# Attention and GEGLU block: the order of the first attention units, and the first gate and value weights loaded by rows

## The chip, the core and the metric

One core of a Trainium2 chip runs the whole program. Its engines are TensorE (PE, with its weight loads listed apart as PEld), VectorE (DVE), ScalarE (ACT), GpSimd (POOL) and SyncE (SP); SP, ACT and POOL also hand transfers to the core's 16 DMA engines. The metric is the device time of one execution in microseconds (us).

## The reference

Eight batches of 576 tokens go through sliding-window attention with eight heads of width 64. Heads 0 to 3 see the last 32 positions ("plain"), heads 4 to 7 every fourth of the last 128 ("dilated"). The result, 4608 tokens of width 512, is the input of a GEGLU block.

```python
scores = scale * np.matmul(q, k.transpose(0, 1, 3, 2))
mask_plain = (rel >= 0) & (rel < window)                                             # window 32
mask_dil = (rel >= 0) & (rel < window * dilation) & (rel % dilation == 0)            # dilation 4
scores = np.where(masks[None, :, :, :], scores, -1000000000.0)
attn = np.exp(scores - max);  attn = attn / (sum(attn) + 1e-09)
x = np.matmul(attn, v).transpose(0, 2, 1, 3).reshape(B * S, H * D)
out = (gelu(x @ w_gate) * (x @ w_val)) @ w_out        # 512 -> 1536 -> 512, gelu with erf
```

## The kernel before

**Tiling.** A "unit" of attention is a pair of heads of one batch, so a batch has four: units 0 and 1 are plain, 2 and 3 dilated. Its steps are named by letters in strings that `run_program` reads one after another; each engine runs what it is given in that order, and nothing is moved by a scheduler. `c` casts q or k, `t` transposes them on PE and copies the result out of PSUM, `b` writes the mask as a bias into PSUM, `S` adds the scores, `P` takes the exponential on ACT, `D` sums it over the keys (matmuls with ones), `N` multiplies it with v, `X` (L608) multiplies N with the reciprocal of D and writes rows of xT, the transposed FFN input. The reciprocal is made in one of two ways: `T` and `B` (two 32x32 stream transposes and a reciprocal on DVE), or `l` and `r`, together `A` (logarithm and exponential of its negative, on ACT). `W` is a filler matmul that nobody reads. Of a word like `D2@20` the number behind `D` is the unit, and the one behind `@` tells the PSUM bank and the place in it.

**FFN.** Tokens come in nine chunks of 512. A chunk has 12 units of 128 hidden columns (nb); each takes four matmuls (kc = 0 to 3, by the 128 rows of xT) for the gate and four for the value (L617). `g` is the gelu on ACT (L776), `u` the product on DVE (L781). A digit word issues so many FFN matmuls from the chunk's list. xT[kc] is written by attention unit kc, so kc = 0, 1, 2, 3 need L608 of units 0, 1, 2, 3. The order of the first sixteen matmuls of chunk 0 (nb, gate or value, kc) is written out:

```python
orders = { 0: "000 100 002 102 010 110 012 112 001 101 011 111 003 103 013 113", ...
```

**Weights and v.** Gate and value weights are loaded in four parts each, by columns: 0 to 255, 256 to 511, and two of 512. POOL hands them to DMA and casts to half precision on the way (`load_w`), through the same instruction queue on which it casts v: v of units 0 and 1 of batch 0 comes by SP into `stage`, and POOL casts it into `vdiag`, where each head's values stand in one half of 128 columns and zeros, written by `zero` on DVE, in the other. One matmul with 128 columns of weights so serves both heads (L441), where units 2 and 3 use pairs of matmuls on a quarter of the array each (L452). POOL's transfers share eight semaphores; a transfer waits until the one eight before it has landed.

After the two batches' inputs and the three output weight tiles, chunk 0's second half (`out_words`) mixes the output matmuls (L624) with the attention of batch 1. From there on attention of the next batch always runs between output matmuls.

Of the kernel before, what the change touches and what calls it, by code (L numbers as in the profile page):

```python
# [9 lines left out]
F16 = mybir.dt.float16  # L10
F32 = mybir.dt.float32
# [10 lines left out]
def kernel(  # L22
# [23 lines left out]
    NKC = DM // P  # L46
# [5 lines left out]
    NB2 = S // BK  # L52
# [5 lines left out]
    const = ctx.enter_context(tc.tile_pool(name="const", bufs=1))  # L58
# [1 line left out]
    ldp = ctx.enter_context(tc.tile_pool(name="ldp", bufs=1))  # L60
    prb = ctx.enter_context(tc.tile_pool(name="prb", bufs=6))
    nrm = ctx.enter_context(tc.tile_pool(name="nrm", bufs=2))
    ffn = ctx.enter_context(tc.tile_pool(name="ffn", bufs=3))
    osbp = ctx.enter_context(tc.tile_pool(name="osbp", bufs=4))

    ones = const.tile([P, CH], F16, tag="ones")
# [7 lines left out]
    class_of = const.tile([P, 4], F16, tag="class_of")  # L74
    late_of = const.tile([P, P], F16, tag="late_of")

    WC = [(0, 256), (256, 512), (512, 1024), (1024, 1536)]
    wg_t = [const.tile([P, NKC, b - a], F16, tag=f"wg{i}", name=f"wg{i}") for i, (a, b) in enumerate(WC)]
    wv_t = [const.tile([P, NKC, b - a], F16, tag=f"wv{i}", name=f"wv{i}") for i, (a, b) in enumerate(WC)]
    wo_t = [const.tile([P, 4, DM], F16, tag=f"wo{i}", name=f"wo{i}") for i in range(3)]  # L80
    xT = [const.tile([P, NT], F16, tag=f"xT{i}", name=f"xT{i}") for i in range(NKC)]

    vraw = [const.tile([P, 4 * NB2 * D], F16, tag=f"v{i}", name=f"v{i}") for i in range(3)]
    vdiag = const.tile([P, 2 * NB2 * P], F16, tag="vdiag")
    qraw = [const.tile([P, 2 * QK], F16, tag=f"q{i}", name=f"q{i}") for i in range(2)]
    stage = const.tile([P, 3840], F32, tag="stage")
    s16 = const.tile([P, 4608], F16, tag="s16")
# [3 lines left out]
    ps = psum.tile([P, 8, 512], F32, tag="ps")  # L91
# [53 lines left out]
        rest_mask(nc.vector, rest)  # L145
        nc.vector.tensor_scalar(rest, rest, 1.0, BIG, ALU.subtract, ALU.mult)

    def load_w(*parts):

        for i in parts:  # L150
            for t, w in ((wg_t, moe_w_gate), (wv_t, moe_w_val)):
                src = w[:, WC[i][0] : WC[i][1]].rearrange("(kc p) n -> p kc n", p=P)
                nc.gpsimd.dma_start(out=t[i], in_=src)

    def load_wo(i):
        return nc.gpsimd.dma_start(
# [11 lines left out]
    def rows_in(src, r):  # L168

        return src.rearrange("h (p r) d -> p h (r d)", r=r)  # L170
# [15 lines left out]
    def at2(t, c0, dims):  # L186
        base = t[:, c0 : c0 + 1]
        return bass.AP(tensor=base.tensor, offset=base.offset, ap=[base.ap[0]] + dims)

    diag = vdiag.rearrange("p (e c) -> p e c", c=P)  # L190

    def zero():

        for x in range(2):
            nc.vector.memset(at2(vdiag[64 * x : 64 * x + 64].bitcast(F32), 32 - 32 * x, [[64, 2 * NB2], [1, 32]]), 0.0)

    def st_of(i):
        return stage[:, 1280 * i : 1280 * i + 1280]
# [48 lines left out]

        return nc.gpsimd.tensor_copy(dst, st_of(i)[:, 0:1152].rearrange("p (e d) -> p e d", d=D))  # L248

    def cast_diag(g):  # L250

        st = st_of(0)[:, 0:1152].rearrange("p (e d) -> p e d", d=D)
        at = slice(NB2 * g, NB2 * g + NB2)
        for x in range(2):
            nc.gpsimd.tensor_copy(diag[half_of(x), at, half_of(x)], st[half_of(x), at])

    def half_of(x, swap=0):
        y = x ^ (1 if swap else 0)
        return slice(64 * y, 64 * y + 64)

    def odd(n):

        return n % 2 if n >= NHP else 0
# [137 lines left out]
    def win(n, at):  # L401

        bank, kind = at // 10, at % 10
        return 512 * bank + ((0, 832, 960, 0) if is_plain(n) else (80, 880, 880, 64))[kind]
# [34 lines left out]
    def emit(mms):  # L439
        for o, lhs, rhs, st, end in mms:  # L440
            nc.tensor.matmul(o, lhs, rhs, start=st, stop=end, skip_group_check=True)  # L441

    def emit_tiles(*lists):

        queues, at = [list(mms) for mms, _ in lists], [0.0] * len(lists)
        while any(queues):
            i = min((i for i in range(len(lists)) if queues[i]), key=lambda i: at[i])
            o, lhs, rhs, st, end = queues[i].pop(0)
            at[i] += max(int(np.prod(rhs.shape[1:])), 72)
            for x in range(2):  # L450
                rows, cols = half_of(x), half_of(x, lists[i][1])
                nc.tensor.matmul(o[cols], lhs[rows], rhs[rows], start=st, stop=end, skip_group_check=True)  # L452
# [91 lines left out]
    def two_num_mms(n, i):  # L544
        b, hp = n // NHP, n % 2
        _, _, _, _, vp, vd = tiles["two", b]
        tiles["num", n] = win(n, i)
        if is_plain(n):
            vp = vp if b else diag
            return two_mms(n, win(n, i), lambda e: vp[:, NB2 * hp + e, :])  # L550
        return two_mms(n, win(n, i), lambda e: vd[:, NB2 * hp + (8 if e is None else e % 2 * 4 + e // 2), :])

    def two_den(n, i):
# [5 lines left out]

    def two_num(n, i):  # L560
        mms = two_num_mms(n, i)
        if n < NHP and is_plain(n):
            emit(mms)
        else:
            emit_tiles((mms, odd(n)))
# [44 lines left out]
    def ffn1_part(c, nb, gi, bank, kcs):  # L610

        tok = slice(c * CH, (c + 1) * CH)
        i = next(i for i, (_, end) in enumerate(WC) if nb * P < end)
        ns = slice(nb * P - WC[i][0], nb * P - WC[i][0] + P)
        w = (wg_t, wv_t)[gi][i]
        for kc, first, end in kcs:
            nc.tensor.matmul(ps[:, bank, :], w[:, kc, ns], xT[kc][:, tok], start=first, stop=end)  # L617

    def parts_of(order):
        return [(kc, i == 0, i == len(order) - 1) for i, kc in enumerate(order)]  # L620
# [41 lines left out]
    def warm(n, bank, rows=P, cols=CH):  # L662

        for _ in range(n):
            nc.tensor.matmul(ps[0:rows, bank, 0:cols], ones[:, 0:rows], ones[:, 0:cols], start=True, stop=True)
# [14 lines left out]
    for h in range(0, HK, 2):  # L680
        for t, src, eng in ((0, q, nc.sync), (1, k, nc.scalar)):
            first = eng.dma_start(out=first_p[:, t, h : h + 2], in_=rows_in(src[0, h : h + 2], 6))
# [9 lines left out]
    v_cast(0, 1)  # L692
    tiles["two", 0] = views(0)

    warm(69, 7, 32, 32)
    warm(4, 7)
    nc.vector.tensor_reduce(class_of, ident.rearrange("p (i r) -> p r i", r=4), axis=mybir.AxisListType.X, op=ALU.max)
    biases()
    zero()
    bias_first(0, 4)  # L700
    load_w(0, 1)
    for g in range(2):
        cast_diag(g)
    load_w(2)

    def second():
# [17 lines left out]
    def gate_banks(c, nb):  # L724

        if c == 0:
            return ((4, 5), (6, 7))[nb] if nb < 2 else ((0, 1), (2, 3))[nb % 2]
        return ((0, 7), (1, 6) if c == 1 else (1, 4))[nb % 2]

    def gate_list(c):  # L730

        if c in firsts:
            first, seen = [], {}
            for word in firsts[c].split():
                nb, gi, kc = (int(x) for x in word)
                i = seen[nb, gi] = seen.get((nb, gi), 0) + 1
                first.append((nb, gi, (kc, i == 1, i == NKC)))
        else:
            first = [(nb, gi, part) for nb in range(2) for gi in range(2) for part in parts_of(range(NKC))]
        order = [(nb, gi) for nb in range(2, NNB) for gi in range(2)]  # L740
        if c == 0:
            order = [(nb + n, gi) for nb in range(2, 10, 2) for gi in range(2) for n in range(2)] + order[16:]
        rest = [(nb, gi, part) for nb, gi in order for part in parts_of(range(NKC))]
        return [lambda m=m: ffn1_part(c, m[0], m[1], gate_banks(c, m[0])[m[1]], [m[2]]) for m in first + rest]

# [60 lines left out]
    def gate_words(c):  # L806

        if c == 0:
            return (
# [4 lines left out]
            )  # L814
        loads = {1: "F3", 2: "R", 3: "F5 H5", 4: "F6 H6", 5: "F7 H7"}.get(c, "")
        rest = " ".join(f"4 g{nb} 4 u{nb}" for nb in range(2, NNB - 1))
        if c == 1:
            return f"{loads} 8 G 3 g0 1 u0 3 g1 1 u1 {rest} 4 g{NNB - 1} 4"
        before = f"e3@{c - 1}" if c < NCH - 1 else ""
        return f"{before} {loads} 7 G 3 g0 1 u0 1 g1 4 u1 {rest} 4 g{NNB - 1} 4" + (f" u{NNB - 1}" if c > 6 else "")  # L820

    def out_words(c):
# [16 lines left out]
        )  # L839

    orders = {
# [43 lines left out]
```

## Time and profile before

| what | before |
|---|---|
| device time, median of 3 | 327.19 us (327.05 to 327.22) |
| the profiled execution, its device time | 326.98 us |
| its span, first to last instruction | 325.3 us |
| granted TensorE clock over the span | 1.000 |
| DVE busy | 150.2 us, 46% |
| ACT busy | 159.6 us, 49% |
| instructions of PE's matmul row | 3207 |
| first FFN matmul starts | 17.74 us |
| fifth FFN matmul starts, the first with value weights | 19.05 us |
| the last of the four L608 of batch 0 ends | 20.40 us |

Times within an execution count from the span's start. The profile page gives each engine's busy time, the span in 40 slices of 8.1 us with the granted clock (PEclk) and the share of DMA in tenths, and the chain of work that ended last. The timeline lists instructions in order: start, duration, engine, source line, operation, tiles written and read, how many, and in brackets how long the engine sat idle before and what ended that. The profiled execution is one of its own, so its device time differs a little from the median; the step from its span to its device time is what lies around the program's first and last instruction.

### The profile page before, as it was taken

The numbers are of one execution on the slowest core, as the hardware profiler recorded it, in microseconds if no ns is written. First come the engines' busy times: TensorE is split into PE (matmuls) and PEld (weight loads), VectorE is DVE, ScalarE is ACT, GpSimd is POOL, SyncE is SP. The second block draws the span as 40 slices with busy tenths as digits, with TensorE's granted clock in tenths as the row PEclk, the third lists the DMA queues.
The fourth block names the chain that finished last, engine by engine and source line by source line (L and its number), as shares of the span: only waits on it lengthen the run. The fifth ranks groups of instructions, "written<-read, shape, count | busy, mean of one in ns | idle before, by whom it ended". The sixth has DMA issues, their size and how long they took to land.

```text
span 325.3 us, 7737 instructions
## 1 busy us (share of the span) xinstructions
PE 318.9 (98%) x3207; PEld 155.8 (48%) x3207; DVE 150.2 (46%) x226; ACT 159.6 (49%) x240; POOL 82.3 (25%) x134
## 2 busy tenths in 40 slices
PE   6999999999999999999999999999999999999996
PEld 4754544445444445445444544445444544444443
DVE  6864636444644464346533554355434644204410
ACT  2662577435753556346633863376435753233321
POOL 8785603402482512332033201411000000000000
PEclk9999999999999999999999999999999999999999
DMA  8999998988799999897489537972000200020002
GB/s 190 188 188 206 201 191 165 269 180 199 171 271 208 240 169 245 197 222 191 119 201 232 141 104 157 253 173 90 32 2 8 94 33 0 2 99 30 0 34 97
DMA packets 106659, 47.11 MB, mean 145 GB/s; under 512 B 83584, under 2 KB 102144, under 8 KB 106624
## 3 DMA queue, kind: packets, MB, share of 16 engines
q1 hardware_dynamic: 93120, 38.29, 50.0%
q0 software_dynamic: 12944, 7.67, 16.7%
q10 hardware_dynamic: 560, 0.66, 0.7%
q8 instruction: 25, 0.41, 0.6%
q14 instruction: 10, 0.08, 0.1%
HBM read 37.75 MB, written 9.44 MB: 145 GB/s over the span
## 4 chain that ended last, share of the span: by engine, by line
PE 61%; ACT 0%; DVE 0%; issue 0%; ACTq 0%
PE ps L617 38%; PE ps L624 19%; PE ps L452 3%; PE ps L648 1%; ACT lg L579 0%; DVE osb L657 0%; ACTq L579 0%
## 5 line engine op out<-in xcount | busy, mean ns | idle before, releaser
L781 DVE SCALAR_TENSOR_TENSOR u_all<-g,ps 128x512 f16<-128x512 f16 x108 | 74.2, 688 | 110.0 <-PE ps L617 93.3
L776 ACT ACTIVATE g<-ps 128x512 f16<-128x512 f32 x108 | 63.6, 597 | 104.1 <-PE ps L617 104.1
L617 PE MATMUL ps<-xT,wg 128*128 128x512 f16 x432 | 112.5, 379 | 0.3 <-DMA wg<-in_moe_w_gate_dram 0.3
L617 PE MATMUL ps<-xT,wv 128*128 128x512 f16 x432 | 112.3, 379 | 0.0
L624 PE MATMUL ps<-wo,u_all 128*128 128x512 f16 x420 | 96.3, 380 | 0.0
L617 PEld LDWEIGHTS <-wv 128*128 128x128 f16 x432 | 42.1, 98 | 51.1 <-DMA wv<-in_moe_w_val_dram 0.7
L617 PEld LDWEIGHTS <-wg 128*128 128x128 f16 x432 | 42.1, 98 | 50.7 <-DMA wg<-in_moe_w_gate_dram 0.4
L624 PEld LDWEIGHTS <-u_all 128*128 128x128 f16 x420 | 39.1, 98 | 45.5 <-issue 0.5
L608 DVE TENSOR_TENSOR xT<-ps,rb 128x576 f16<-128x576 f32 x32 | 28.8, 938 | 16.9 <-PE ps L452 13.6
L482 ACT ACTIVATE P<-ps 128x832 f16<-128x832 f32 (+1 forms) x32 | 25.3, 835 | 15.4 <-PE ps L452 15.3
L211 POOL CAST s<-stage 128x640 f16<-128x640 f32 x24 | 17.4, 752 | 51.0 <-DMA stage<-in_q_dram 37.9
L248 POOL CAST v<-stage 128x1152 f16<-128x1152 f32 x11 | 12.7, 1151 | 63.0 <-DMA stage<-in_v_dram 47.4
L579 ACT ACTIVATE lg<-ps 128x576 f32<-128x576 f32 x30 | 18.7, 653 | 11.6 <-DVE xT L608 9.0
L637 DVE TENSOR_SCALAR osb<-ps 128x512 f32<-128x512 f32 x22 | 15.1, 686 | 12.2 <-PE ps L624 11.6
L585 ACT ACTIVATE rb<-lg 128x576 f32<-128x576 f32 x30 | 19.5, 690 | 0.3
L635 ACT ACTIVATE osb<-ps 128x512 f32<-128x512 f32 x13 | 7.8, 598 | 21.2 <-PE ps L624 21.2
L223 POOL CAST s<-stage 128x512 f16<-128x512 f32 x24 | 14.4, 627 | 10.1 <-DMA stage<-in_q_dram 7.9
L487 DVE TENSOR_TENSOR P<-P,two_d 128x768 f16<-128x768 f16 x14 | 9.4, 678 | 9.8 <-ACT P L482 9.1
L487 DVE TENSOR_TENSOR P<-P,two_p 128x832 f16<-128x832 f16 x14 | 8.6, 612 | 9.5 <-ACT P L482 9.5
L803 ACT ACT_TABLE_LOAD x9 | 11.5, 1283 | 0.2
L452 PEld LDWEIGHTS <-v 64*64 64x64 f16 x616 | 7.6, 107 | 6.3 <-issue 5.7
L452 PEld LDWEIGHTS <-q 64*64 64x64 f16 x576 | 7.9, 107 | 5.0 <-issue 3.0
(67 smaller groups left out, 135.6 us busy)
## 6 DMA issues: line engine op xcount, KB each, us to landing
out_dram<-osb SPq DMA_DIRECT2D x35, 256.0 KB, 2.8
stage<-in_v_dram SPq DMA_DIRECT2D x28, 144.0 KB, 3.8
stage<-in_q_dram SPq DMA_DIRECT2D x24, 128.0 KB, 3.6
stage<-in_k_dram SPq DMA_DIRECT2D x24, 128.0 KB, 2.9
stage<-in_q_dram SPq DMA_DIRECT2D x6, 512.0 KB, 4.7
stage<-in_k_dram SPq DMA_DIRECT2D x6, 512.0 KB, 5.3
stage<-in_v_dram SPq DMA_DIRECT2D x20, 128.0 KB, 2.8
wo<-in_moe_w_out_dram POOLq DMA_DIRECT2D x3, 512.0 KB, 16.8
```

The source lines that it names most:

```text
L211: nc.gpsimd.tensor_copy(s16[:, 1280 * t + 640 * g : 1280 * t + 640 * g + 640].rearrange("p (k c) -> p k c", k=5), st_of(i).rearrange("p (k ...
L452: nc.tensor.matmul(o[cols], lhs[rows], rhs[rows], start=st, stop=end, skip_group_check=True)
L482: nc.scalar.activation(pt[:, 0 : src.shape[1]], src, AF.Exp, bias=0.0, scale=scale)
L487: tiles["M"] = nc.vector.tensor_tensor(pt, pt, mask, ALU.mult)
L579: nc.scalar.activation(lg, psf[:, c0 : c0 + S], AF.Ln)
L585: nc.scalar.activation(rb, tiles.pop(("lg", n)), AF.Exp, scale=-1.0)
L608: nc.vector.tensor_tensor(dst, num, rb, ALU.mult)
L617: nc.tensor.matmul(ps[:, bank, :], w[:, kc, ns], xT[kc][:, tok], start=first, stop=end)
L624: nc.tensor.matmul(ps[:, bank, :], u_all[:, fc, tb * P : (tb + 1) * P], wo_t[fc // 4][:, fc % 4, :], start=(fc == 0), stop=(fc == NNB - 1),)
L637: nc.vector.tensor_scalar(osb, ps[:, bank, :], 1.0 / USCALE, None, ALU.mult)
L776: nc.scalar.activation(g, ps[:, gate_banks(c, args[0])[0], :], AF.Gelu)
L781: nc.vector.scalar_tensor_tensor(u_all[:, nb, :], tiles.pop(("g", nb)), USCALE, val, ALU.mult, ALU.mult)
```

## The change

Four things change, all in the work ahead of and inside the first chunk.

1. The words of chunk 0 are in another order: casts and transposes of unit 0 and 1's second tensors (`c2 c3 t2 t3`) and of unit 2 come together, before the sums of unit 0; unit 3's sums, logarithm and reciprocal come ahead of the values of units 0, 2 and 3; L608 runs for units 0, 2, 3, 1. Unit 1's reciprocal goes from `T`, `B` to `l`, `r`. Eleven of twelve filler matmuls go. The warm-up is 46 matmuls of 32 columns and 12 of 64 where it was 69 of 32.
2. v of unit 0 is cast densely (one cast), and its values use pairs of matmuls as units 2 and 3 do; only unit 1 keeps `vdiag`, which is half as large, and so is what `zero` clears.
3. The first 512 columns of the gate and value weights come by rows: gate rows of kc = 0 and kc = 2 in a transfer each (256 KB of the 4-byte source each), value rows of kc = 0 and 2, then gate rows of 1 and 3, then value rows of 1 and 3. On POOL's queue the cast of unit 0's v stands between the first value and the second gate part, the casts of unit 1's v before the second value part.
4. The written order of chunk 0 covers the first four units: gate of units 0 to 3 comes before the value of units 2 and 3; their PSUM banks change, and g has four buffers where it had three.

```diff
-    ffn = ctx.enter_context(tc.tile_pool(name="ffn", bufs=3))
+    ffn = ctx.enter_context(tc.tile_pool(name="ffn", bufs=4))
...
-    WC = [(0, 256), (256, 512), (512, 1024), (1024, 1536)]
...
+    wg_t = [const.tile([P, NKC // (1 if i > 1 else 2), CH], F16, tag=f"wg{i}", name=f"wg{i}") for i in range(4)]
+    wg_t[0] = [const.tile([P, CH], F16, tag=f"wg0{i}", name=f"wg0{i}") for i in range(2)]
+    wv_t = [const.tile([P, NKC // (1 if i > 1 else 2), CH], F16, tag=f"wv{i}", name=f"wv{i}") for i in range(4)]
...
-    vdiag = const.tile([P, 2 * NB2 * P], F16, tag="vdiag")
+    vdiag = const.tile([P, NB2 * P], F16, tag="vdiag")
...
+    def load_w(i, *kinds):
+
+        for gi in kinds or (0, 1):
+            t, w = ((wg_t, moe_w_gate), (wv_t, moe_w_val))[gi]
+            cols = w[:, CH * max(i - 1, 0) : CH * max(i - 1, 0) + CH]
+            if i > 1:
+                nc.gpsimd.dma_start(out=t[i], in_=cols.rearrange("(kc p) n -> p kc n", p=P))
+            elif i == 0 and gi == 0:
+                for n in range(2):
+                    nc.gpsimd.dma_start(out=t[i][n], in_=cols[2 * n * P : 2 * n * P + P, :])
+            else:
+                nc.gpsimd.dma_start(out=t[i], in_=cols.rearrange("(a b p) n -> b p a n", b=2, p=P)[i])
...
-            nc.vector.memset(at2(vdiag[64 * x : 64 * x + 64].bitcast(F32), 32 - 32 * x, [[64, 2 * NB2], [1, 32]]), 0.0)
+            nc.vector.memset(at2(vdiag[64 * x : 64 * x + 64].bitcast(F32), 32 - 32 * x, [[64, NB2], [1, 32]]), 0.0)
...
-    def cast_diag(g):
...
+    def cast_first(g):
+
+        if g == 0:
+            nc.gpsimd.tensor_copy(vraw[0][:, 0:576], st_of(0)[:, 0:576])
+            return
+        st = st_of(0)[:, 576:1152].rearrange("p (e d) -> p e d", d=D)
         for x in range(2):
-            nc.gpsimd.tensor_copy(diag[half_of(x), at, half_of(x)], st[half_of(x), at])
+            nc.gpsimd.tensor_copy(diag[half_of(x), :, half_of(x)], st[half_of(x)])
...
-    warm(69, 7, 32, 32)
+    warm(46, 7, 32, 32)
+    warm(12, 7, 32, 64)
     warm(4, 7)
...
-    load_w(0, 1)
-    for g in range(2):
-        cast_diag(g)
+    load_w(0)
+    cast_first(0)
+    load_w(1, 0)
+    cast_first(1)
+    load_w(1, 1)
     load_w(2)
...
-            return ((4, 5), (6, 7))[nb] if nb < 2 else ((0, 1), (2, 3))[nb % 2]
+            return ((4, 2), (5, 3), (6, 7), (0, 1))[nb] if nb < 4 else ((0, 1), (2, 3))[nb % 2]
...
-                "c0@0 c1@0 t0@0@1 t1@1@0 b1@6 W1@3@0 S0@4 P0 t4@0@1 W1@3@0 c2@0 c3@0 t5@1@0 t2@2@1 t3@3@0 D0@40 T0 B0 "
-                "t6@1@1 W10@7 t7@0@0 S1@6 P1 b2@2 S2@2 P2 D1@60 T1 B1 b3@0 S3@0 P3 D2@20 A2 N0@40 X0 D3@00 N2@60 X2 A3 N3@20 1 "
-                "N1@00 X1 X3 G V 15 g0 u0 g1 u1 4 g2 4 g3 4 u2 4 u3 4 g4 4 g5 4 u4 4 u5 4 g6 4 g7 4 u6 4 u7 4 g8 4 g9 4 u8 3 "
+                "c0@0 c1@0 t0@0@1 t1@1@0 b1@6 W1@3@0 S0@4 P0 c2@0 c3@0 t4@0@1 t2@2@0 t3@3@1 t5@1@0 D0@40 T0 B0 S1@6 P1 b2@2 S2@2 P2 "
+                "t6@0@1 t7@1@0 D1@60 l1 r1 b3@0 S3@0 P3 D2@20 l2 r2 D3@00 l3 r3 N0@40 X0 N2@20 X2 N3@60 X3 2 N1@00 X1 G V 11 g0 1 g1 4 g2 2 g3 3 u0 1 u1 4 u2 4 u3 "
+                "4 g4 4 g5 4 u4 4 u5 4 g6 4 g7 4 u6 4 u7 4 g8 4 g9 4 u8 3 "
...
-        0: "000 100 002 102 010 110 012 112 001 101 011 111 003 103 013 113",
+        0: "000 100 002 102 010 110 012 112 200 202 003 103 001 101 300 302 203 201 303 301 013 113 011 111",
```

Behind the written order the value matmuls of units 2 and 3 follow, and from unit 4 on the list is as before. Everything after chunk 0's first half stands in the same order in both kernels.

More of the change, by code (lines that the diff above doesn't have):

```diff
@@ L75 @@
     late_of = const.tile([P, P], F16, tag="late_of")
-    WC = [(0, 256), (256, 512), (512, 1024), (1024, 1536)]
-    wg_t = [const.tile([P, NKC, b - a], F16, tag=f"wg{i}", name=f"wg{i}") for i, (a, b) in enumerate(WC)]
-    wv_t = [const.tile([P, NKC, b - a], F16, tag=f"wv{i}", name=f"wv{i}") for i, (a, b) in enumerate(WC)]
+    wg_t = [const.tile([P, NKC // (1 if i > 1 else 2), CH], F16, tag=f"wg{i}", name=f"wg{i}") for i in range(4)]
+    wg_t[0] = [const.tile([P, CH], F16, tag=f"wg0{i}", name=f"wg0{i}") for i in range(2)]
+    wv_t = [const.tile([P, NKC // (1 if i > 1 else 2), CH], F16, tag=f"wv{i}", name=f"wv{i}") for i in range(4)]
     wo_t = [const.tile([P, 4, DM], F16, tag=f"wo{i}", name=f"wo{i}") for i in range(3)]
@@ L146, in biases @@
         nc.vector.tensor_scalar(rest, rest, 1.0, BIG, ALU.subtract, ALU.mult)
[L148 to L153, printed above, removed]
+    def load_w(i, *kinds):
[9 more added lines that the diff above has]
+                nc.gpsimd.dma_start(out=t[i], in_=cols.rearrange("(a b p) n -> b p a n", b=2, p=P)[i])
     def load_wo(i):
@@ L248, in cast_v @@
         return nc.gpsimd.tensor_copy(dst, st_of(i)[:, 0:1152].rearrange("p (e d) -> p e d", d=D))
-    def cast_diag(g):
-        st = st_of(0)[:, 0:1152].rearrange("p (e d) -> p e d", d=D)
-        at = slice(NB2 * g, NB2 * g + NB2)
+    def cast_first(g):
[3 more added lines that the diff above has]
+        st = st_of(0)[:, 576:1152].rearrange("p (e d) -> p e d", d=D)
         for x in range(2):
-            nc.gpsimd.tensor_copy(diag[half_of(x), at, half_of(x)], st[half_of(x), at])
+            nc.gpsimd.tensor_copy(diag[half_of(x), :, half_of(x)], st[half_of(x)])
     def half_of(x, swap=0):
@@ L548, in two_num_mms @@
         if is_plain(n):
-            vp = vp if b else diag
-            return two_mms(n, win(n, i), lambda e: vp[:, NB2 * hp + e, :])
+            return two_mms(n, win(n, i), lambda e: diag[:, e, :] if n == 1 else vp[:, NB2 * hp + e, :])
         return two_mms(n, win(n, i), lambda e: vd[:, NB2 * hp + (8 if e is None else e % 2 * 4 + e // 2), :])
@@ L561, in two_num @@
         mms = two_num_mms(n, i)
-        if n < NHP and is_plain(n):
+        if n == 1:
             emit(mms)
@@ L612, in ffn1_part @@
         tok = slice(c * CH, (c + 1) * CH)
-        i = next(i for i, (_, end) in enumerate(WC) if nb * P < end)
-        ns = slice(nb * P - WC[i][0], nb * P - WC[i][0] + P)
-        w = (wg_t, wv_t)[gi][i]
+        ns = slice(nb % 4 * P, nb % 4 * P + P)
+        ws = (wg_t, wv_t)[gi]
         for kc, first, end in kcs:
-            nc.tensor.matmul(ps[:, bank, :], w[:, kc, ns], xT[kc][:, tok], start=first, stop=end)
+            w = ws[nb // 4 + 1][:, kc] if nb > 3 else (ws[0][kc // 2] if kc % 2 + gi == 0 else ws[kc % 2][:, kc // 2])
+            nc.tensor.matmul(ps[:, bank, :], w[:, ns], xT[kc][:, tok], start=first, stop=end)
     def parts_of(order):
@@ L737, in gate_list @@
                 first.append((nb, gi, (kc, i == 1, i == NKC)))
+            assert set(seen.values()) == {NKC}
         else:
@@ L741, in gate_list @@
         if c == 0:
-            order = [(nb + n, gi) for nb in range(2, 10, 2) for gi in range(2) for n in range(2)] + order[16:]
+            order = [(2, 1), (3, 1)] + [(nb + n, gi) for nb in range(4, 10, 2) for gi in range(2) for n in range(2)] + order[16:]
         rest = [(nb, gi, part) for nb, gi in order for part in parts_of(range(NKC))]
```

## The prediction

> **What bounds the kernel now.** First the busy table, the row of slices and the chain that ended last.
>
> ```profile
> PE 318.9 (98%) x3207; PEld 155.8 (48%) x3207; DVE 150.2 (46%) x226; ACT 159.6 (49%) x240; POOL 82.3 (25%) x134
> ...
> PEclk9999999999999999999999999999999999999999
> DMA  8999998988799999897489537972000200020002
> ...
> PE 61%; ACT 0%; DVE 0%; issue 0%; ACTq 0%
> PE ps L617 38%; PE ps L624 19%; PE ps L452 3%; PE ps L648 1%; ACT lg L579 0%; DVE osb L657 0%; ACTq L579 0%
> ```
>
> The chain is matmuls alone. It goes back only to 122 us, where one wait cuts it, so I looked further back in the order of instructions. From 19.05 us to the end one matmul of 512 columns follows another every 0.2158 us; all that is lost is some 0.09 us where the array changes tile shape, and 0.3 us at 122.4. Nothing behind 19 us can be gained by this change; it can only move the point where that stream opens, or tear a hole into it. So the stretch around the opening decides.
>
> ```profile
> 15.69 0.44 PEld L441 LDWEIGHTS <-vdiag 128*128 128x128 f16 x10 [0.38 <-POOL vdiag L255]
> ...
> 17.67 0.74 POOL L153 DMA_DIRECT2D wg<-in_moe_w_gate_dram  x1
> 17.73 0.10 PEld L617 LDWEIGHTS <-wg 128*128 128x128 f16 x1 [0.39 <-DMA wg<-in_moe_w_gate_dram]
> 17.74 0.39 PE L617 MATMUL ps<-xT,wg 128*128 128x512 f16 x1 [0.30 <-DMA wg<-in_moe_w_gate_dram]
> ...
> 18.36 0.81 PE L617 MATMUL ps<-xT,wg 128*128 128x512 f16 x3
> ...
> 18.60 1.79 DVE L608 TENSOR_TENSOR xT<-ps,rb 128x576 f16<-128x576 f32 x2 [0.30 <-PE ps L441]
> 19.05 0.55 PEld L617 LDWEIGHTS <-wv 128*128 128x128 f16 x4 [0.38 <-DMA wv<-in_moe_w_val_dram]
> ...
> 26.82 1.42 PEld L617 LDWEIGHTS <-wv 128*128 128x128 f16 x8 [0.31 <-DMA wv<-in_moe_w_val_dram]
> 26.84 1.89 PE L617 MATMUL ps<-xT,wv 128*128 128x512 f16 x8
> ```
>
> The reader is to see three waits for weights: the first gate weights (17.7), the first value weights (19.05, the fifth FFN matmul), and the third value part wv2 (26.82, the 41st), where only the load of weights waits. The attention (L608) is no longer what is waited for at 19.05. The landing events in the trace say the same: wg0 17.69, wv0 19.01, wg1 20.32, wv1 21.65, wg2 24.25, wv2 26.77. PE and the weight transfers run neck and neck: 36 matmuls x 0.2158 = 7.77 us from 19.05 give 26.82.
>
> **Attention front.** Replayed with the durations of the timeline:
> - `zero` halves: two memsets of 0.54 us become about 0.28 each. The first cast stood right behind them (5.47), its data landed at 4.82, so unit 0's scores go from 7.86 to about 7.35. This is lost again at unit 2's transposes, which wait for their DMA until 8.44 (idle 0.15 before them now).
> - Order: second pair's casts and transposes ahead, and of 12 filler matmuls (L671: 1 + 1 + 10) one is left, so 0.22 + 0.67 us go. Transposes then end at 9.5, their four copies (0.64 on ACT, 0.76 on DVE, two on each) at 10.2 and 10.8; scores of unit 1 at 10.25 (12.14 before), exp to 11.7; unit 2's exp to 12.6.
> - Unit 1's transposed reciprocal (0.77 + 0.27 + 0.78 on DVE) becomes log and exp on ACT (0.65 + 0.68). ACT then is the attention's engine: copy to 13.1, log and exp of unit 1 to 14.45, exp of unit 3 to 15.27 (15.83 before), logs and exps of unit 2 to 16.5 and of unit 3 to 17.8 (18.34 before).
> - Unit 0's v dense: 10 matmuls 128x96 (0.40 us) become 20 half-array ones (40 take 0.75, so 0.37): nothing. On POOL two 64x576 casts (0.68, 0.66) become one 128x576 (about 0.70, by 0.75 for 128x640). It needs the stage's second piece, behind which today's second cast starts at 14.98; so values of unit 0 start at 15.74 (15.69 now).
> - L608 runs in the order 0, 2, 3, 1: 16.35 to 17.1 (0.76 us, a plain one), to 18.16 (1.13, a dilated one), to 19.2, to 19.9. All four ended at 20.40 before. The matmuls of chunk 0 need pair 2 as third and fourth: 18.22; so the fifth could start at 18.65.
>
> All this gains 0.4 us at the fifth matmul, **if the weights were there**.
>
> **Weights.** The first four FFN matmuls still need gate weights only, and the fifth still a value part, with which 512 KB (as landed) are in, as now. So its landing doesn't come nearer by the split. Packets grow from 512 B to 1 KB: in the trace 256 KB of 512 B packets take 1.32 us (the steps between the landings above), 512 KB of 1 KB packets 2.52 to 2.60, so 1.27 per 256 KB. From the last v landing at 16.35: wg first halves 17.0 and 17.6, wv0 18.89, wg1 20.16, wv1 21.43. Fifth matmul at 18.93: **-0.12 us** (the 41st then could start at 26.70, -0.14). The rule in the Trainium skill that speaks against splitting (DMA: Bandwidth & Descriptors, "Measured": batch to 1 MiB or more; "Anatomy of one DMA": about 2.0 us fixed per transfer) would put up to 2.0 us on the one transfer more. The row says zero as long as transfers are queued: landings 1.32 apart, without a gap. I take zero there, but the fixed part comes back where the queue runs dry.
>
> And there it can: POOL now casts between the weights. Today all four first parts are handed over by 14.17; only wg2 comes behind the casts (17.67), and the DMA packet records show the price: 95 KB landed per half microsecond, then 41 and 76 KB in those from 19.5 and 20.0, so full rate some 2.1 us after the hand-over and 0.43 us lost on the mean engine. After: wg1 15.65, wv1 17.73 (its two diag casts wait for stage pieces of 16.04 and 17.0 as today), wg2 18.46, wv2 19.20. Most engines end wv0 near 16.95 and idle 0.4 to 0.85 us, then 0.4 to 0.8 before wv1; today's 0.43 goes. They have that to give: 15 of 16 finish wg0 by 16.31, the last at 17.69, and that last engine, 1.4 us behind all through, never runs dry. So wv2 lands near 26.55 on the last engine and 26.15 to 26.55 on the rest. PE asks for it at 18.93 + 36 x 0.2158 = 26.70. Bound from below: no hole.
>
> On top comes PE's own instruction fetch (the queue named instruction, 25 packets of 16 KB): one took 0.96 us at 22.99, and one engine's wg2 came 0.8 us behind its neighbours. It follows PE's count of instructions; 12 fewer matmuls ahead of it move it by 12 x 0.216 = 2.6 us to about 25.5, into the tail of wv2, on an engine whose lead is now used up: 26.9 to 27.3. Then the 41st matmul starts at 26.95 to 27.35 against 26.84: **+0.1 to +0.5**. I take 27.05, +0.2, as the fetch may miss wv2.
>
> **The rest.** Order and banks of hidden units (nb) 0 to 3: each bank's former reader (L608 at the latest 19.9; the gate and product rows of 0.60 and 0.69) ends before its next matmul; nb 4's gate in bank 0 at 25.0 wants nb 3's gelu, over by 23.5. The fourth buffer of g removes what the four gates in a row would wait for. Zero. Later weights: wg3 is due at 31.9 (29.27 now), the first output weights at 41.70 (41.37 now): 0.33 us of cover, the thinnest; the fetch at 39.21 that delays it also moves back. Warm-up 46 x 27 ns + 12 x 27 to 53 ns is what 69 x 27 ns was, and PE waits behind it anyway.
>
> **Clock.** Taking fillers out speaks against the Trainium skill (TensorE: Matmul & The Clock Gate, last table: no PE gaps over about 3 us; one idle window of 3.4 us halves the clock). My largest gap is 1.1 us (12.3 to 13.46). The row: from 5.3 to 8.7 us matmuls other than transposes fill only 0.9 us and the clock stays at 9; after the change the leanest 3.4 us (12.0 to 15.4) hold 1.37. By the row nothing; if the gate closed, 3.4 us at half rate cost 1.7.
>
> **Sum.** Profiled execution 326.98 (span 325.3, 1.7 around it): -0.14 from the opening, +0.35 at wv2 (27.05 against 26.70), so +0.2, 327.18. The median shown is 0.21 above that execution: **327.4**. A difference under 0.2% (0.65 us) this measurement can't tell from none; that is where I expect it.
>
> **Rivals and chances.**
> - Forecast, weights pace both ends, 326.9 to 327.8: 72%.
> - The lagging engine lags less (its 1.4 us come from the 1.5 us fetch at 9.6, which moves too), the fifth matmul starts at 18.65 and wv2 is in time: -0.4, 326.8; with L608 earlier still, under 326.5. For: attention has slack. Against: fetches keep coming. 9%, half of it beyond 0.2%.
> - Slower: the queue dries out on the lagging engines too. Place: wv1 and wv2; decides once hand-over to full rate is above 2.5 us (wv1 then starts after 20.2, where the last engine ends wg1). With the fetch on top wv2 lands at 27.7 to 28.1: +0.9 to +1.3, 328.3. 14%.
> - Clock gate closes in the front: +1.7, 328.9. 5%.
> Range 326.7 to 328.2: the rest outside is about 2 in 10. Faster 5%, same 76%, slower 19%.
>
> **What would show it.** Right: the fifth FFN matmul waits for wv at 18.8 to 19.0, L608 ends before 20.1, a wait for wv near 26.7 to 27.3. Wrong: the fifth matmul waits for L608; no wait at wv2; a PEclk digit under 9 in the second or third slice; a hole at the first output matmul.

## The result and the profile after

The changed kernel takes **328.09 us** (median of 8 runs, 327.56 to 329.06), the kernel before beside it 327.14 us (8 runs, 326.89 to 327.78): a ratio of 1.0029, with an interval of 1.0019 to 1.0039. That is 0.95 us slower, with the whole interval above 1. The time lies inside the range given, but it is the place and the size of the third rival, not of the forecast. The profiled execution of the changed kernel took 328.04 us, its span is 326.3 us.

The page of the changed kernel first: the busy table, the granted clock and the DMA share in slices, and the chain that ended last, by engine and by line.

```profile
PE 318.6 (98%) x3195; PEld 155.3 (48%) x3195; DVE 148.2 (45%) x223; ACT 160.6 (49%) x242; POOL 81.9 (25%) x134
...
PEclk9999999999999999999999999999999999999999
DMA  8999999998899997896589627972000200020002
...
PE 93%; DMA 4%; DVE 1%; issue 1%; POOL 0%; ACT 0%
```

The source lines have moved: what was L608 (writes of xT) is L615 in the changed kernel, the FFN's L617 is L624, the output matmuls' L624 is L631, and L441 and L452 are L449 and L460 (experiments 2 and 8, on the kernel before, keep the old lines).

PE, DVE and POOL are busy for 0.3 to 2.0 us less than before, ACT for 1.0 us more (unit 1's reciprocal is made there now), and the clock is untouched, so the loss is idle time on PE. What is new is the 4% of DMA in the chain: 9.02 us of it (2.8%) are the transfer of wv2, the rest is a load of q before 8.7 us. Before, the chain was cut at 122 us and held matmuls almost alone; now it can be followed to the start. The chain of waits in order of time (start, length, what) names the new piece:

```profile
17.89 1.11 DVE xT L615
19.00 9.02 DMA wv<-in_moe_w_val_dram
28.07 8.59 PE ps L624 x39
```

From 19.00 to 28.02 the end of the program waits for one transfer: wv2, from POOL's hand-over to its landing. (That a DVE instruction stands before it is inferred by the profile; POOL itself has no idle time there, as its hand-over before took from 18.25 to 19.01.) Behind it PE runs as before. The timeline of the changed kernel (start, duration, engine, line, operation, count, in brackets the idle time before and what ended it) shows how POOL came to hand it over at 19.00, and what PE did meanwhile:

```profile
13.69 0.33 PE L449 MATMUL ps<-P,two_ones 128*128 128x288 f16 x3 [0.77 <-issue]
14.84 0.66 POOL L259 CAST v<-stage 128x576 f16<-128x576 f32 x1 [2.29 <-DMA stage<-in_v_dram]
15.45 0.73 POOL L159 DMA_DIRECT2D wg<-in_moe_w_gate_dram  x1
16.18 1.41 POOL L263 CAST vdiag<-stage 64x576 f16<-64x576 f32 x2
17.21 3.50 DVE L615 TENSOR_TENSOR xT<-ps,rb 128x576 f16<-128x576 f32 x4 [3.55 <-PE ps L460]
17.53 0.72 POOL L159 DMA_DIRECT2D wv<-in_moe_w_val_dram  x1
...
19.00 0.75 POOL L154 DMA_DIRECT2D wv<-in_moe_w_val_dram  x1
19.49 1.02 PE L624 MATMUL ps<-xT,wv 128*128 128x512 f16 x4
...
28.07 0.60 PE L624 MATMUL ps<-xT,wv 128*128 128x512 f16 x2 [0.64 <-DMA wv<-in_moe_w_val_dram]
```

Three things are to be seen. POOL sits 2.29 us in front of the first cast, waiting for v, and behind that cast stand wg1 and, after two more casts, wv1. The fifth FFN matmul starts at 19.49 where it was 19.05. And until 28.07 PE waits for wv2 (the 41st FFN matmul, 26.84 before): 1.23 us later, and the 96th is 1.24 later, the span 1.08.

How much the DMA engines moved in the two stretches in question is in the windows view: stretch, length, busy time and count of PE, PEld, DVE, ACT, POOL, then the clock, the DMA share and GB/s. The kernel before:

```profile
16.50:18.00 1.50, 1.20 (x46) 1.00 (x43) 1.38 (x2) 1.47 (x3) 1.20 (x3) 1.00 1.44 199
18.50:20.00 1.50, 1.50 (x9) 0.57 (x7) 1.40 (x2) 1.14 (x1) 1.50 (x3) 1.00 1.29 155
```

The changed kernel:

```profile
16.50:18.00 1.50, 1.41 (x64) 1.38 (x63) 0.79 (x2) 1.38 (x3) 1.44 (x3) 1.00 0.89 130
18.50:20.00 1.50, 1.44 (x16) 0.87 (x15) 1.50 (x3) 1.48 (x2) 1.50 (x3) 1.00 0.63 73
```

In both stretches the rate is lower than before, 130 against 199 and 73 against 155 GB/s: POOL's transfers had run dry. The packet records of that one queue say the same in KB per half microsecond, and the landing events say what it cost. All 16 DMA engines report each transfer; the median of the 16 tells of the queue, the last of the 16 is what PE waits for.

```
KB per 0.5 us from   16.5 17.0 17.5 18.0 18.5 19.0 19.5 20.0
before                 95   92   95   95   98   93   41   76
changed                54   51   74   97   46   26   38   93

landed, us            wv0          wg1          wv1          wg2          wv2
               median last  median last  median last  median last  median last
before          17.14 19.01  18.46 20.32  19.78 21.65  22.91 24.25  25.52 26.77
changed         17.05 18.86  19.03 20.14  21.44 22.28  24.31 24.82  26.91 28.02
```

Against 95 KB per half microsecond the changed kernel lacks 281 KB, the one before 75 KB. Before, the median engine was 1.25 to 1.87 us ahead of the last one; in the changed kernel that lead melts, and at wg2 it is 0.51.

### The profile page after: what moved, and what is told of

Same layout as the page of the kernel before. It is cut to its first block, busy times and chain, and to the rows that moved or that the text cites. A ratio compares the mean times of both kernels' runs of the same rounds, so it can differ in the third digit from the quotient of the medians.

```text
span 326.3 us, 7703 instructions
## 1 busy us (share of the span) xinstructions
PE 318.6 (98%) x3195; PEld 155.3 (48%) x3195; DVE 148.2 (45%) x223; ACT 160.6 (49%) x242; POOL 81.9 (25%) x134
## 3 DMA queue, kind: packets, MB, share of 16 engines
q0 software_dynamic: 11936, 7.67, 16.5%
## 4 chain that ended last, share of the span: by engine, by line
PE 93%; DMA 4%; DVE 1%; issue 1%; POOL 0%; ACT 0%
PE ps L624 55%; PE ps L631 29%; PE ps L460 6%; DMA wv<-in_moe_w_val_dram 3%; DMA xT<-in_q_dram 2%; PE ps L655 1%; PE ps L380 1%; PE ps L449 1%; DVE xT L615 0%; ACT P L490 0%; PE ps L400 0%; PE ps L434 0%; POOL band L117 0%; PE ps L377 0%; DVE ones L67 0%
## 5 line engine op out<-in xcount | busy, mean ns | idle before, releaser
L624 PE MATMUL ps<-xT,wv 128*128 128x512 f16 x432 | 112.0, 379 | 0.6 <-DMA wv<-in_moe_w_val_dram 0.6
L624 PE MATMUL ps<-xT,wg 128*128 128x512 f16 x432 | 112.2, 379 | 0.2
L631 PE MATMUL ps<-wo,u_all 128*128 128x512 f16 x420 | 96.3, 380 | 0.0
L624 PEld LDWEIGHTS <-wv 128*128 128x128 f16 x432 | 42.2, 98 | 51.8 <-DMA wv<-in_moe_w_val_dram 1.1
L624 PEld LDWEIGHTS <-wg 128*128 128x128 f16 x432 | 42.2, 98 | 50.5 <-issue 0.2
L631 PEld LDWEIGHTS <-u_all 128*128 128x128 f16 x420 | 39.1, 98 | 45.5 <-issue 0.5
L615 DVE TENSOR_TENSOR xT<-ps,rb 128x576 f16<-128x576 f32 x32 | 28.6, 938 | 19.7 <-PE ps L460 17.1
L586 ACT ACTIVATE lg<-ps 128x576 f32<-128x576 f32 x31 | 19.4, 652 | 12.1 <-DVE xT L615 8.7
L592 ACT ACTIVATE rb<-lg 128x576 f32<-128x576 f32 x31 | 20.2, 690 | 0.5 <-DVE xT L615 0.2
L460 PEld LDWEIGHTS <-v 64*64 64x64 f16 x636 | 8.0, 107 | 6.1 <-issue 5.9
L460 PEld LDWEIGHTS <-q 64*64 64x64 f16 x576 | 7.8, 107 | 5.0 <-issue 3.8
```

Of the source, the lines that this page charges most:

```text
L586: nc.scalar.activation(lg, psf[:, c0 : c0 + S], AF.Ln)
L592: nc.scalar.activation(rb, tiles.pop(("lg", n)), AF.Exp, scale=-1.0)
L615: nc.vector.tensor_tensor(dst, num, rb, ALU.mult)
L624: nc.tensor.matmul(ps[:, bank, :], w[:, ns], xT[kc][:, tok], start=first, stop=end)
L631: nc.tensor.matmul(ps[:, bank, :], u_all[:, fc, tb * P : (tb + 1) * P], wo_t[fc // 4][:, fc % 4, :], start=(fc == 0), stop=(fc == NNB - 1),)
```

## The experiments

Six theories were in play, with these names. **Queue (Q):** the casts between the hand-overs let POOL's DMA queue run dry twice. **Front (F):** the new order of the attention makes the opening late. **Rows (R):** loading by rows, with one transfer more, is itself slower. **Instruction fetch (I):** PE's third fetch of instructions, now at 24.64 instead of 22.99, falls into the tail of wv2. **PE stall (P):** with some 12 matmuls fewer ahead of the first scores, PE gets to the end of its instructions on hand before the first fetch is in; the 0.77 us before 13.69 above, behind PE's 223rd matmul, has no other cause in the profile. **Clock (C):** in some executions TensorE's clock drops, as the fillers are gone. Q, F, R and I were there first, P and C came from what those runs showed. The kernel before was run beside them each time: medians 327.09 us (experiments 1 to 4), 327.15 (5 to 8) and 327.13 (9 to 11), of 44 to 53 runs each.

**1. Casts behind the hand-overs (Q undone).** The changed kernel with all first parts handed over before the first cast:

```diff
     load_w(0)
+    load_w(1)
     cast_first(0)
-    load_w(1, 0)
     cast_first(1)
-    load_w(1, 1)
     load_w(2)
```

> The changed kernel with all four first weight parts handed over ahead of POOL's casts of v; nothing else. Theory Q (POOL's casts between the weights let the software DMA queue run dry twice, which makes wv2 late): no half microsecond under 80 KB between 16.5 and 19 us, wv2 lands by 27.0 instead of 28.02, the 41st FFN matmul follows the fifth (19.49) without a hole at 27.26, time 327.3. Theory F (the new attention order is what makes it late, the fifth matmul at 19.49 against 19.05): the fifth matmul stays, and the time falls only by what lies between 28.06 and 27.26. Rival R (weights by rows, or one transfer more, are slower in themselves): wv2 stays near 28, time 328.1.

Measured: 327.73 us (22 runs), ratio 1.0021 [1.0012, 1.0031]. The same two stretches of its profile:

```profile
16.50:18.00 1.50, 1.50 (x66) 1.44 (x65) 0.52 (x1) 1.47 (x3) 1.44 (x3) 1.00 1.27 213
18.50:20.00 1.50, 1.43 (x16) 0.85 (x15) 1.50 (x2) 1.48 (x2) 1.50 (x3) 1.00 1.20 165
```

The first dry stretch is gone and the second is no deeper than in the kernel before (165 against 155 GB/s), wv2 lands at 25.24 on the median engine and 26.42 on the last, and the 41st matmul waits for nothing. But it starts at 27.53, not at 26.8: the fifth starts at 19.76, with the stall behind the 223rd matmul (from its start at 12.62 to the next at 13.95). So the queue's hole is repaired, and behind it the late front comes to light. The median gives back only 0.36 of the 0.95 us, and the intervals of the two kernels overlap: the trace shows the repair, the time alone does not. In 7 of the 22 executions the mean granted clock is 0.995, and those took 328.48 to 328.86; the median of the other 15 is 327.52.

**2. Casts between, in the kernel before (Q alone).**

```diff
-    load_w(0, 1)
-    for g in range(2):
-        cast_diag(g)
+    load_w(0)
+    cast_diag(0)
+    load_w(1, kinds=(0,))
+    cast_diag(1)
+    load_w(1, kinds=(1,))
     load_w(2)
```

> The kernel before with one part of the change alone: its first weight parts, by columns as they were, are handed over in the changed kernel's places among the casts (wg0, wv0, two casts, wg1, two casts, wv1). Theory Q: the queue runs dry near 17 and 19 us, wv2 lands 0.6 to 1.2 us later than 26.77, time 327.7 to 328.3. Theories F and R: 327.1 as before.

Measured: 328.96 us (7 runs), ratio 1.0046 [1.0030, 1.0062]: more than expected. From its timeline:

```profile
15.67 0.74 POOL L153 DMA_DIRECT2D wg<-in_moe_w_gate_dram  x1
16.45 1.45 POOL L255 CAST vdiag<-stage 64x576 f16<-64x576 f32 x2
17.84 0.74 POOL L153 DMA_DIRECT2D wv<-in_moe_w_val_dram  x1
...
26.49 1.90 PE L617 MATMUL ps<-xT,wg 128*128 128x512 f16 x8 [1.00 <-DMA wg<-in_moe_w_gate_dram]
...
28.99 1.25 PE L617 MATMUL ps<-xT,wv 128*128 128x512 f16 x5 [0.60 <-DMA wv<-in_moe_w_val_dram]
```

The hand-overs stand 0.2 to 0.3 us behind those of the changed kernel, and the queue moves 24 KB in the half microsecond from 17.0 and 25 in that from 19.5. Two holes follow, at wg2 and at wv2 (which lands at 28.95). This one edit, without any other part of the change, makes a kernel whose median is 0.87 us above that of the whole change (the intervals of the ratios still overlap a little). Why it costs about twice as much was not separated further; its transfers are by columns, and between 20.0 and 21.5 its queue moved 66 to 80 KB per half microsecond where the changed kernel's moved 89 to 97.

**3. The old order of the attention in the changed kernel (F undone).**

```diff
-"... S0@4 P0 c2@0 c3@0 t4@0@1 t2@2@0 t3@3@1 t5@1@0 D0@40 T0 B0 S1@6 P1 b2@2 S2@2 P2 t6@0@1 t7@1@0 D1@60 l1 r1 b3@0 S3@0 P3 D2@20 l2 r2 D3@00 l3 r3 N0@40 X0 N2@20 X2 N3@60 X3 2 N1@00 X1 ..."
+"... S0@4 P0 t4@0@1 W1@3@0 c2@0 c3@0 t5@1@0 t2@2@1 t3@3@0 D0@40 T0 B0 t6@1@1 W10@7 t7@0@0 S1@6 P1 b2@2 S2@2 P2 D1@60 T1 B1 b3@0 S3@0 P3 D2@20 A2 N0@40 X0 D3@00 N2@20 X2 A3 N3@60 2 N1@00 X3 X1 ..."
```

> The changed kernel with the attention order, the fillers and unit 1's reciprocal of before; weights, casts, dense v and the FFN order as changed. Theory Q: the fifth FFN matmul comes at about 19.0 again, and the wait for wv2 grows from 0.8 to some 1.2 us; time stays at 328.1. Theory F: the time falls by the 0.44 us of the fifth matmul or more, to 327.6 or less.

Measured: 328.26 us (6 runs), ratio 1.0038 [1.0023, 1.0053]. The fifth matmul starts at 18.80, 0.69 us earlier than in the changed kernel, and it gains nothing: PE waits at the 33rd (to 25.52) and again at the 41st, to 28.10, because wv2's landing is where it was (26.91 on the median engine, 28.06 on the last):

```profile
28.10 1.90 PE L624 MATMUL ps<-xT,wv 128*128 128x512 f16 x8 [0.69 <-DMA wv<-in_moe_w_val_dram]
```

F falls as the cause of the loss.

**4. Twelve more warm-up matmuls (I, and later P).** In the changed kernel:

```diff
-    warm(46, 7, 32, 32)
+    warm(58, 7, 32, 32)
     warm(12, 7, 32, 64)
```

> The changed kernel with 12 more warm-up matmuls of 32 columns, so that PE's count of instructions is that of before. Theory I (the instruction fetch at 24.64, moved by the 12 missing matmuls, sits in the tail of wv2): the third fetch comes at about 22 to 23 again, wv2's last engine lands near 27.4 instead of 28.02, time 327.5. Theory Q alone, without the fetch: wv2 stays near 28, time 328.1. The stall of 0.8 us of PE at 12.9, for which the profile shows no cause, should go or move if it is the second block of instructions that PE waits for there.

Measured: 328.14 us (22 runs, 326.69 to 329.67), ratio 1.0028 [1.0018, 1.0039]: no better than the changed kernel. The count of matmuls alone doesn't mend it. The execution that was profiled is the quickest of them (326.69 us) and speaks for itself alone: its fetches came early (8.33, 14.62, 18.35), there is no stall behind the 223rd matmul, the fifth FFN matmul started at 18.54, and the queue still moved only 44, 28 and 31 KB in the half microseconds from 18.0. But v came earlier in it: POOL's first cast waited only until 13.99, wv2 was handed over at 18.50 and was in at 26.59 on the last engine, so the 41st matmul, possible at 18.54 + 7.77 = 26.31, started at 26.63. In this one execution the dry queue cost 0.32 us there. Why this kernel's times spread over 3 us was not found.

**5. Both: casts behind the hand-overs, and twelve more warm-ups (Q and P undone).**

> The changed kernel with both repairs: all four first weight parts ahead of POOL's casts, and 12 more warm-up matmuls. Theory Q plus theory P (PE stands still at its 223rd matmul because, with 12 matmuls fewer ahead of the first scores, the fetch of its next block of instructions starts only behind those scores): no dry spell, no stall of 0.8 to 1.1 us at 12.6, fifth matmul at 18.6 to 18.9, time 326.8 to 327.1, at or a little below before. If the stall is not the fetch: it stays at the place where D of unit 1 stands, the fifth matmul stays near 19.5, time 327.5 to 327.7.

Measured: **327.00 us** (13 runs), ratio 0.9998 [0.9988, 1.0008]. The whole loss is gone. In its timeline PE goes through the place of the stall without a gap:

```profile
12.97 0.53 PE L449 MATMUL ps<-P,two_ones 128*128 128x384 f16 x5
```

The fifth matmul starts at 19.01 and the 41st at 27.18, where it still waits 0.24 us for wv2. The weights still come by rows, in one transfer more, and the kernel is level with the one before: R falls.

**6. Casts behind the hand-overs, with the old attention order** (the edits of 1 and 3).

> The changed kernel with all four first weight parts ahead of the casts and the attention order, fillers and unit 1's reciprocal of before; weights by rows, dense v and the FFN order as changed. Theory Q: with the dry spells gone and the front as before the time is that of before or 0.1 us less, 327.0. Rival R (the weights by rows or the order of the hidden units cost something in themselves): 327.5 or more. Theory C (with fillers gone the clock gate closes in some executions): none with a mean clock of 0.995 here, where the loads-ahead kernel had 7 of 22.

Measured: 327.24 us (21 runs), ratio 1.0006 [0.9999, 1.0013]. It has the stall (13.35 to 14.22) and the fifth matmul at 19.57, but no hole behind it (41st at 27.34), and no execution with a clock of 0.995. Against experiment 3 the queue alone is worth 1.0 us here.

**7. The changed kernel again**, for a second trace of it.

> The changed kernel once more, unaltered, beside the others on the same chip. All theories: 328.1. It shows how far the time and the instruction fetches of one program differ from one execution to the next, and whether the stall at PE's 223rd matmul and the dry spells near 17 and 19 us are there again: theories Q and P say both are.

Measured: 328.09 us (9 runs), ratio 1.0031 [1.0020, 1.0042]. In the profiled execution PE's stall is short (12.61 to 13.13, from start to start), so the front is on time:

```profile
27.79 1.90 PE L624 MATMUL ps<-xT,wv 128*128 128x512 f16 x8 [0.92 <-DMA wv<-in_moe_w_val_dram]
```

The fifth matmul started at 18.93, as the prediction had it, and PE could have taken the 41st at 18.93 + 7.77 = 26.70. It had to wait for wv2 to 27.79. In both of its traces the changed kernel is bound by its weights, with a late front (19.49) and without one.

**8. Twelve warm-ups fewer, in the kernel before (P alone).** `warm(69, ...)` becomes `warm(57, ...)`.

> The kernel before with 12 fewer warm-up matmuls (57 of 69) and nothing else. Theory P: the first fetch starts behind the first scores, near 10.5 instead of 9.6, and PE stands still for some 0.5 to 1.2 us at its 223rd matmul, then some 12.5 us into the span; the fifth FFN matmul moves from 19.05 to 19.3 to 19.8 and the time to 327.4 to 327.9. If fetches don't matter: 327.1, as warm-ups ahead of a wait cost nothing.

Measured: 327.25 us (21 runs), ratio 1.0006 [0.9999, 1.0012]. The stall appears behind the same 223rd matmul, now among other instructions, which speaks for PE's count rather than for what it waits for:

```profile
13.12 0.39 PE L452 MATMUL ps<-q 64*64 64x96 f16 x10
13.95 0.32 PE L452 MATMUL ps<-q 64*64 64x80 f16 x8 [0.43 <-issue]
```

The first fetch comes at 11.13 instead of 9.60, the fifth matmul at 19.50, the 41st at 27.27 and the span ends 0.24 later. The mechanism of P is there; its price over many runs is 0.1 us, which can't be told from nothing, and the expectation of 327.4 or more was wrong.

**9. As 5, with wg2 ahead of the casts too:** `load_w(2, 0)` before `cast_first(0)`, `load_w(2, 1)` after the casts.

> The loads-ahead kernel with 12 more warm-ups, and the third gate part (wg2) ahead of the casts as well. Theory Q: the dip that is left at 19.5 us (39 KB in half a microsecond) goes, wv2 lands before 26.5, the 41st matmul follows the fifth by 7.77 us without a hole; fifth at 18.5 to 19.0, time 326.6 to 326.9, 0.1% below before. If something else holds the fifth matmul: 327.0, as without it.

Measured: 327.11 us (13 runs), ratio 1.0000 [0.9993, 1.0008]. The queue has no dip at all:

```profile
18.50:20.00 1.50, 1.43 (x14) 0.74 (x11) 1.50 (x3) 1.31 (x2) 1.50 (x3) 1.00 1.23 202
```

No wait at the 41st matmul (27.04) and wv2 in at 26.79, but it is no quicker than before: the fifth starts at 19.27, since wv0 itself landed at 19.14. With the queue always full, the opening of this execution is bound by the transfers that precede wv0.

**10. One dry spell.** The changed kernel with `load_w(1, 1)` ahead of `cast_first(1)`, so that only unit 0's cast stands between:

> The changed kernel with the second value part ahead of the casts of unit 1's v; the cast of unit 0's v stays between the first and the second pair of parts. Theory Q: the dry spell near 17 us stays, the one near 19 shrinks to the one of before; wv2 lands 0.3 to 0.7 us earlier than in the changed kernel, time 327.4 to 327.9, between the changed kernel and the loads-ahead one. Rival: 328.1.

Measured: 327.54 us (22 runs), ratio 1.0018 [1.0008, 1.0028]. The first spell stays (62, 47 and 68 KB per half microsecond from 16.5), the second is gone (92, 88, 103 from 18.5). wv1 lands at 20.57 on the median engine (21.44 in the changed kernel), wv2 at 26.00 (26.91). On the last engine wv2 gains less, 27.81 against 28.02, and the wait before the 41st matmul shrinks to 0.19 us:

```profile
27.86 1.90 PE L624 MATMUL ps<-xT,wv 128*128 128x512 f16 x8 [0.19 <-DMA wv<-in_moe_w_val_dram]
```

In the medians more than half of the loss (0.55 of 0.95) goes with the second spell, though the intervals of the two kernels overlap. It can't be told from experiment 1 by its time; both have a late front (fifth matmul at 19.74 and 19.76). 5 of the 22 executions have a clock of 0.995 (328.40 to 329.48).

**11. The old attention order with the queue full:** experiment 6 with eleven more warm-ups and wg2 ahead of the casts.

> As e9, but with the attention order, fillers and unit 1's reciprocal of before, and PE's count of instructions ahead of the first scores as before. Theory Q plus P: no stall, no dry spell, fifth matmul at 18.8 to 19.0, time 326.8 to 327.0. Against e9 it shows what the new attention order is worth by itself once nothing else is in its way: 0 to 0.3 us.

Measured: 327.76 us (22 runs), ratio 1.0013 [1.0007, 1.0020], slower than 9 by 0.65. What the hand-over of wg2 pushes back now is the cast that the old order asks for at once:

```profile
15.06 0.77 POOL L154 DMA_DIRECT2D wg<-in_moe_w_gate_dram  x1 [0.41 <-DMA v<-in_v_dram]
15.82 0.68 POOL L259 CAST v<-stage 128x576 f16<-128x576 f32 x1
...
16.55 0.58 PE L460 MATMUL ps<-P,v 64*64 64x96 f16 x20 [0.92 <-POOL v L259]
```

In the old order the values of unit 0 follow directly on unit 2's sums, and PE stands for 0.92 us. The new order puts unit 3's sums in between, and in experiment 9 the same push costs nothing. That is a use of the new order: it takes a later v.

## Why the prediction was off

**What held.** Behind 19 us there was nothing to gain. The opening hung on the weights: wv0 landed at 18.86 (18.89 predicted), wg1 at 20.14 (20.16). POOL's hand-overs came at 15.45, 17.53, 18.25 and 19.00 against 15.65, 17.73, 18.46 and 19.20. The queue ran dry at the two places named, and the 41st matmul waited for wv2. Banks, the written order and g's buffers cost nothing that a trace shows. In experiment 7's execution the fifth matmul came at 18.93, as predicted.

**The step that failed** is a term of the sum: "full rate some 2.1 us after the hand-over", with its conclusion that the last engine "never runs dry". The 2.1 was read off the sum over all engines, where 41 and 76 KB in two half microseconds look like a restart. The same packets in steps of 0.1 us are at their lowest, 3 KB, at 19.8, 2.1 us after the hand-over, and reach the full 19 KB again at 20.3, 2.6 us after it. The landings of the median engine in the same trace of before agree with the larger value. wg2 was handed over at 17.67 and was in at 22.91; less the 2.55 us that it takes, its transfer counts as begun at 20.36, 2.69 us after the hand-over. In the changed kernel wg1 gives 19.03 - 1.27 - 15.45 = 2.31 us and wv1 21.44 - 1.27 - 17.53 = 2.64 us; wg1 of experiment 10 gives 2.65. The Trainium skill (DMA: Bandwidth & Descriptors, "Anatomy of one DMA") has about 2.0 us as the fixed part of a transfer from this engine; these rows lie 0.3 to 0.7 above it. The prediction weighed that fixed part against the one additional transfer, where landings 1.27 to 1.32 us apart show that queued transfers hide it. It counts where the queue is empty at the hand-over, and that is also where the smaller value was used.

With 2.69 the forecast's own sum turns over. wv1 would start at 17.73 + 2.69 = 20.42, behind the 20.16 at which the last engine ends wg1: the point from which the third rival was to decide (2.5 us) is passed. Measured, the median engine began wv1 at 21.44 - 1.27 = 20.17 and the last had ended wg1 at 20.14. The median engine idled 17.76 - 17.05 = 0.71 and 20.17 - 19.03 = 1.14 us, where "0.4 to 0.85" and "0.4 to 0.8" were expected, and 0.58 us before (the prediction had 0.43). It ends wv2 1.39 us later than before (26.91 against 25.52) and has no lead left to give. The second spell is the mis-sized one, and the median of experiment 10 points to it as the one that costs more.

**The fetch** was put into wv2's tail at about 25.5; it came at 24.64, and one engine landed wv2 at 28.02 where the next to last had it at 27.36. So in that execution it may have added up to 0.66 us. It isn't needed for the loss: in experiment 3 two engines are that late (28.00 and 28.06), and experiment 4, which moves the count, keeps the loss in its median. What it adds to the medians was not separated.

**The front** was predicted at 18.65 and came at 19.49 in the profiled execution. One of the prediction's own signs of being wrong came with it: the fifth matmul didn't wait for wv0 (in at 18.86) but followed the attention. L608 of unit 2 (L615 now) ends at 19.01, the third and fourth matmul start behind it at 19.06, the fifth after them, and the last L608 ends at 20.71, not before 20.1. The first cast waited for its data until 5.12 (4.82 was assumed), and PE stalled for 0.77 us behind its 223rd matmul. The prediction moved the later fetch by twelve matmuls; of the first it said, in its second rival, that it moves too, and asked what that does to the lagging DMA engine but not what it does to PE. It moved from 9.60 to 10.88. In the changed kernel wv2 hides this (experiments 3 and 7). Once the queue is mended it is what is left: with the new order, experiment 1 against 5 is 0.73 us for twelve small matmuls (0.52 without the executions of experiment 1 at a clock of 0.995). That isn't the stall alone, for in the kernel before and with the old order it costs about 0.1 (experiments 8 and 6).

**The chances** were the wrong way round: 72% for a loss that the lead absorbs, 14% for the rival, which named the place (wv1 and wv2), the range of the landing (27.7 to 28.1; measured 28.02 and 27.74) and the price (+0.9 to +1.3; +1.23 at the 41st matmul, +0.95 in the medians). That the range up to 328.2 holds 328.09 is luck: the forecast's own span ended at 327.8, and the rival that came true was put at 328.3, just outside the range.

**Nothing here beats the kernel before.** Experiments 5 and 9 mend the change and end level with it (0.9998 and 1.0000).

**Open** is where the clock drops in the executions at 0.995, what the rest of the 0.73 us between experiments 1 and 5 is, how much of the loss is the fetch's, and why experiment 4 spreads.

## What to carry to other kernels

Before a cast is put between two transfers on the engine that issues both, ask when its data comes and how long the queue still has work at that moment: here a cast that waited for v held back the transfers behind it, and each restart took 2.3 to 2.7 us from the hand-over, counted back from the landing, while transfers queued in time landed 1.27 to 1.32 us apart. Read such a restart from the landings of the median engine, not from half microseconds of a rate summed over all of them, and check whether a lead that you mean to spend is still there after the first spell. And where warm-up or filler matmuls go, count what else follows the number of instructions: a fetch, a stall and the clock can move with them.

## What the hardware showed that was not expected

**A stall at a count of instructions.** In the changed kernel and experiments 1, 6, 7, 8 and 10 PE takes 0.5 to 1.3 us from the start of its 223rd matmul to the next one, whatever these two are, with no semaphore to wait for; in experiment 3 it takes 0.3. In the kernel before and experiments 2, 4, 5, 9 and 11, which have eleven or more warm-ups more, it takes at most 0.17. It goes with the first fetch of instructions (a packet of 16 KB on the instruction queue), which starts at 10.5 to 11.3 us where there is a stall and at 8.3 to 10.2 where there is none. In the seven traces with a stall the 224th matmul starts 1.38 to 1.68 us after the end of that packet, and in none of the thirteen traces does it start sooner. That fits a PE that waits for the fetch; that it does so is still inferred.

**The clock without a long gap.** A mean granted clock of 0.995, and about 1.1 us more, occurs in 7 of 22 and 5 of 22 executions of experiments 1 and 10, and in 1 of 17 of the changed kernel: kernels with the new order and 46 + 12 warm-ups. It occurs in none of experiments 4, 5, 6, 8, 9 and 11 (13 to 22 runs each), which have the old order or more warm-ups. Over a span of 326 us, 0.5% would be 3.3 us at half rate (an estimate). The Trainium skill (TensorE: Matmul & The Clock Gate, last table) asks for no PE gap over about 3 us; the longest in these traces behind the start of the warm-up is 1.15 us (experiment 1). No profiled execution was one of these, so where the clock drops isn't shown; the fourth rival (+1.7) may be this, at a smaller price and in few executions.
